# A fused attention and gated-MLP kernel: casts and copies moved to ScalarE, loads in another turn, and a first quarter of products issued one by one

## The chip, the cores and the metric

The kernel runs on one core of one Trainium2 chip. Its metric is the device time of one launch in microseconds (us), smaller is better. A core has five engines that run their own queues of instructions and wait for each other by semaphores: PE (TensorE, matrix products; PEld is its loading of weights), ACT (ScalarE), DVE (VectorE), POOL (GpSimd), and SP (SyncE), which here only issues DMAs.

## What is computed

A windowed attention with four sink keys, then an MLP with a gate, on 4 x 768 tokens of 8 heads x 64:

```
scores = q @ k.T / sqrt(64);  keep = (key < 4) or (0 <= row - key < 128)
a = softmax(where(keep, scores, -1e9));  attn = a @ v          # per batch and head
x = attn as (3072 tokens, 512)
h = x @ w_in                                                    # w_in: 512 x 2048
g = h * sigmoid(beta * h)
out = g @ w_out                                                 # w_out: 2048 x 512
```

The kernel computes in bf16 with f32 sums, and the sigmoid as a tanh: g = (tanh(beta h / 2) + 1) * h, with the half put into the last copy.

## The kernel before

**The tiling.** The tokens are cut into 8 blocks of 384 (`TT`). A *unit* n (0 to 31) is the attention of one pair of heads for one block: units 4T to 4T + 3 make the block T of x, kept turned in `xT`. A *tile* i (0 to 127) is one 128 x 384 piece of h: tile i belongs to block i // 16 and is the sum of four products (c = 0 to 3), one for each unit of its block. So "tiles 0 to 15" are block 0 and need units 0 to 3 and all of w_in; tiles 16 to 31 are block 1 and need units 4 to 7. After each tile come a tanh on ACT (`tanh`, L755) and a gate on DVE (`gate`, L769); a PSUM bank is free again when its gate is done. Tiles 4 to 15 take turns in two banks (`acc0`, `acc1`), later ones in four. The output products (`project`, L796) of block 0 begin when tile 31 has been issued, and from then on tiles and output products of neighbouring blocks are mixed.

**A unit's steps.** SP loads q, k and v (f32) into `q_stage`, `k_stage`, `v_stage`. POOL casts them to bf16 (`cast`, L490 and L493, 384 columns each). For units 0 to 11 PE turns q and k ("in", `transpose_in`, L513), and one copy of 768 columns brings them out of PSUM to `qkT` (L522). From unit 12 on a DMA does it. Then: the scores of the sink keys ("sink", L542) with an exp to `E_sink` (L545); the scores in two chunks ("a" and "b", `scores`, L569), each with an exp of 768 columns to `E` (L576) and a mask by DVE (`mask`, L587); a @ v ("av", `attend`, L685 and L696); 1/sum and its product (`normalise`, L705 and L707); and the way out to `xT` ("out", `transpose_out`: PE L724, a copy of 384 columns L728). For n below `ADDED` = 6 the mask is not multiplied by DVE but added on PE, by a product of a unit matrix with `far_a` or `far_b` ahead of the scores (L561, two products of 384 columns for a chunk).

**The weights.** w_in comes in pieces 0 to 7 of 0.5 MB (`load_w`, L473): pieces 2j and 2j + 1 hold rows c = 0, 1 and c = 2, 3 of the columns that tiles 4j to 4j + 3 of each block need. POOL casts each to bf16 (`cast_w`, L478, 1024 columns). w_out follows in eight pieces in the same buffers `wst`.

**What sets the order.** The program is recorded as nodes and a list scheduler (`Prog.order`) places them: at each step it takes, on each engine, the node that could start first by the costs given with each `op` (`busy`, `lag`), with some look ahead; ties go to the node recorded first. `P.together` makes one node of several instructions. So the order of recording, the costs and the dependencies decide every engine's queue; at run time the queues are fixed. The order of recording is a loop over slots s: slot s records tile s (0 to 31), and the steps of units whose place is s. `EARLY` gives the places of the steps of units 4 to 7 (fractions lie between tiles), `FIRST` those of units 8 on: a unit's steps are at FIRST[n] + 0, 1, 2, 3, 5, 7 (`STEPS`). SP's loads are recorded in a line: units 0 to 3, w_in pieces 0 to 3, units 4 to 7, w_in pieces 4 to 7, units 8 to 11, w_out. `at` sets the slots after which the whole loads of later units are issued. `BANK_B` and `BANK_S` say in which PSUM bank the second chunk and the sink scores of units 4 to 7 go.

A tile is recorded so:

```
def hidden(i):
    with P.together("pe"):
        for c in range(3 if i < 4 else 0, 4):
            node = hidden_matmul(i, c)
    tanh(i)
    return node
```

Tiles 0 to 3 had their products c = 0 to 2 recorded singly before, as units 0 to 2 come. Each product waits for its piece of w_in and its unit's part of xT:

```
r=[("w_in", m // 4 * 2 + c // 2), ("xT", T, c)]
```

Of the kernel before, what the change touches and what calls it, by code (L numbers as in the profile page):

```python
# [17 lines left out]
TT = 384  # L18
# [5 lines left out]
NW = 8  # L24
# [15 lines left out]
S_PIPE = 3 * NM  # L40
S_END = S_PIPE + (NT - 2) * NM

EARLY = {4: {'in': 0.2, 'sink': 3.0, 'a': 3.4, 'b': 5.0, 'av': 5.6, 'out': 8.0},
# [3 lines left out]
BANK_B = {4: 'h', 5: 's', 6: 'h', 7: 's'}  # L47
BANK_S = {4: 'h', 5: 'h', 6: 'h', 7: 'h'}

FIRST = {8: 27, 9: 33, 10: 34, 11: 38}  # L50
FIRST.update({12: 44, 13: 47, 14: 50, 15: 53, 16: 60, 17: 60})
FIRST.update({n: 68 + 8 * (n // 2 - 9) for n in range(18, NU)})
TURN = 0

XBAR, WHOLE = 12, 16

ADDED, FAR = 6, -float(1 << 20)
LATE, PAIRED = 2, 16
STEPS = {0: "in", 1: "sink", 2: "a", 3: "b", 5: "av", 7: "out"}

# [227 lines left out]
def bass_streamingllm_window__then__act_swish_beta_kernel(  # L288
# [71 lines left out]
    def pe(n):  # L360
        return {"busy": 2.5 + n / 2.4, "lag": 260.0}
# [89 lines left out]
    def load(n):  # L451
        for name in "qkv":
            if name != "v" and n < XBAR:
                load_qk(n, name)
            else:
                load_head(n, name, 0)
                load_head(n, name, 1)
# [17 lines left out]

    def cast_w(i):
        view, _, dst = w_piece(i)
        op("gp", lambda e: e.tensor_copy(dst, view), r=[("wst", i % NW)],  # L478
           w=[("w_in" if i < NW else "w_out", i % NW)], busy=985.0, lag=100.0)

    def cast(n, first=False):
        _, _, half, pb = place(n)
        z = n % NQK

        def view(name):
            return stage[name][pb][:, :, 3 * half:3 * half + 3, :].rearrange("p h c d -> p c h d")

        for x, name in enumerate("qk"):
            eng = "dve" if first and name == "k" else "gp"
            op(eng, lambda e, x=x, name=name: e.tensor_copy(qk16[z][:, x, :, :, :], view(name)),  # L490
               r=[(name + "_stage", pb, half, hh) for hh in range(2)], w=[(name + "16", z)],
               busy=451.0, lag=100.0)
        op("gp", lambda e: e.tensor_copy(v_aug[pb][:, 3 * half:3 * half + 3, :, 0:D], view("v")),  # L493
           r=[("v_stage", pb, half, hh) for hh in range(2)], w=[("v_aug", pb, half)], busy=451.0,
           lag=100.0)
        if n >= XBAR:
            op("sp", lambda e: e.dma_start_transpose(
                qkT[pb][:, half, :, :].rearrange("p w (c x) -> p (w c) x", c=3),
                qk16[z][:, :, :, :, :].rearrange("p w c h d -> p (w c h d)")),
               r=[("q16", z), ("k16", z)], w=[("qT", pb, half), ("qkT", pb, half)], dma=f"t{pb}{half}",  # L500
               **transfer(2 * TT * 256, 240, 1400.0))
# [50 lines left out]
    def scores(n, c, bank, name):  # L552
        _, _, half, pb = place(n)
        at = 0
        if n < ADDED:
            w = width(half, c)
            far, tile = (far_a, "far_a") if (half, c) == (0, 0) else (far_b, "far_b")
            first = 128 if (half, c) == (1, 0) else 0
            with P.together("pe"):
                for hh in range(2):  # L560
                    op("pe", lambda e, hh=hh, w=w: e.matmul(  # L561
                        bank[:, hh, 0:w], ident[:, :], far[:, first:first + w], start=True, stop=False,
                        skip_group_check=True), r=["ident", tile], w=[f"{name}{hh}"], **pe(w))
        with P.together("pe"):
            for kb, qb, nq in CHUNKS[half][c]:
                w = 128 * nq
                for hh in range(2):
                    rows = slice(64 * hh, 64 * hh + 64)
                    op("pe", lambda e, at=at, w=w, kb=kb, qb=qb, hh=hh, rows=rows: e.matmul(  # L569
                        bank[:, hh, at:at + w], qkT[pb][rows, kb // 3, 1, kb % 3 * 128:kb % 3 * 128 + 128],  # L570
                        qkT[pb][rows, half, 0, qb % 3 * 128:qb % 3 * 128 + w], start=n >= ADDED,
                        stop=True, skip_group_check=n < ADDED),
                       r=[("qT", pb, half), ("qkT", pb, kb // 3)], w=[f"{name}{hh}"],
                       busy=50.0 + w / 4.8, lag=260.0)
                at += w
        op("act", lambda e: e.activation(E[n % 2][:, c, :, 0:at], bank[:, 0:2, 0:at], AF.Exp,  # L576
                                         bias=0.0, scale=SCALE),
           x=[f"{name}0", f"{name}1"], w=[("E", n % 2, c)], **act(768))

    def mask(n, c):  # L580
        if n < ADDED:
            return
        half = place(n)[2]
        w = width(half, c)
        m, names = (mask_a, MASK_A) if (half, c) == (0, 0) else (mask_b, MASK_B)
        first = 128 if (half, c) == (1, 0) else 0
        op("dve", lambda e: e.tensor_tensor(  # L587
            E[n % 2][:, c, :, 0:w], E[n % 2][:, c, :, 0:w],
            m[:, first:first + w].unsqueeze(1).to_broadcast([128, 2, w]), ALU.mult),
           r=[("E", n % 2, c), *names], w=[("E", n % 2, c)], **dve(780.0))  # L590
# [153 lines left out]
    def hidden_matmul(i, c):  # L744
        T, m = i // NM, i % NM
        bank, name = hidden_bank(i)
        return op("pe", lambda e: e.matmul(  # L747
            bank, w_in16[:, c, m * 128:(m + 1) * 128], xT[:, c, T * TT:(T + 1) * TT],
            start=(c == 0), stop=(c == 3)),
           r=[("w_in", m // 4 * 2 + c // 2), ("xT", T, c)], w=[name], **pe(TT))  # L750

    def tanh(i):
        m = i % NM
# [3 lines left out]
           x=[name], r=["beta"], w=[("th", i % 3)], **act(TT + 100))  # L757

    def hidden(i):
        with P.together("pe"):  # L760
            for c in range(3 if i < 4 else 0, 4):
                node = hidden_matmul(i, c)
        tanh(i)
        return node

# [7 lines left out]
    def project_last(half, m):  # L773
        T, t = NT - 1, 2
        bank, name = (acc[0][:, 0:256], "acc0") if half == 0 else (h_ps[:, 0, 0:256], "h0")
        cols = slice(256 * half, 256 * half + 256)
        node = op("pe", lambda e: e.matmul(bank, g[T % 2][:, m, t * 128:(t + 1) * 128],
                                           w_out16[:, m, cols], start=(m == 0), stop=(m == NM - 1)),
                  r=[("g", T % 2, m), ("w_out", m // 2)], w=[name], **pe(256))
        if m == NM - 1:  # L780
            row = T * TT + t * 128
            if half == 0:
                op("act", lambda e: e.activation(out_sb[3][:, cols], bank, AF.Copy, bias=0.0,
                                                 scale=0.5), x=[name], w=[("out_sb", 3)], **act(256))
            else:
                op("dve", lambda e: e.tensor_scalar(out_sb[0][:, cols], bank, 0.5, None, ALU.mult),
                   x=[name], w=[("out_sb", 0)], **dve(330.0))
            op("sp" if half else "act", lambda e, z=3 * (1 - half): e.dma_start(
                out[row:row + 128, cols], out_sb[z][:, cols]),
               r=[("out_sb", 3 * (1 - half))], dma=f"e{half}", **transfer(128 * 256 * 4, 275))  # L790
        return node
# [3 lines left out]
    def project(T, t, m, bank, name, eng="act"):  # L795
        node = op("pe", lambda e: e.matmul(bank, g[T % 2][:, m, t * 128:(t + 1) * 128],  # L796
                                    w_out16[:, m, :], start=(m == 0), stop=(m == NM - 1)),
           r=[("g", T % 2, m), ("w_out", m // 2)], w=[name], **pe(NOUT))
        if m == NM - 1:
            z = n_out[0] % 4  # L800
            n_out[0] += 1
# [38 lines left out]
    load_w(2)  # L840
    load_w(3)
    load(4)
    load(5)
    load(6)
    load(7)
    load_w(4)
    load_w(5)
    load_w(6)
    load_w(7)
    cast(0, True)  # L850
# [57 lines left out]
        sink_keys(n, ended)  # L908


    at = {16: 38, 17: 46, 18: 52, 19: 57, 24: 69, 25: 75, 26: 81, 27: 87}
    loads = {t + 2 * x: (n, name) for n, t in at.items() for x, name in enumerate("qkv")}
    casts = {FIRST[n - 2] + (3 if n % 2 and n - 2 >= PAIRED else 1): n for n in range(10, NU)}
    casts.update({EARLY[n - 2]["sink"]: n for n in range(6, 8)})
# [1 line left out]
    for s in sorted(slots):  # L916
# [14 lines left out]
        for n, step in here:  # L931
            half = place(n)[2]
            if step == "in" and n < XBAR:
                transpose_in(n, eng="dve")
            if step == "sink" and half == 1:
                scores_sink(n, *((h_ps[:, 0, :], "h0") if BANK_S.get(n) == "h" else (s_ps[:, 0, :], "s0") if n < PAIRED
                                 else (tr_ps, "tr")))
            if step == "b" and XBAR <= n < PAIRED:
                scores_at_once(n)
# [14 lines left out]
                    later.append(lambda n=n, ended=ended: sink_keys(n, ended))  # L954
            if step == "out":
                if n < XBAR:
                    transpose_out(n, eng="act" if n < 8 else "dve")
        if s in casts:
            n = casts[s]
            cast(n)  # L960
# [100 lines left out]
```

## Time and profile before

| | us |
|---|---|
| median of 3 runs | 227.72 (225.61, 227.89, 227.72) |
| the profiled execution | 226.35 |
| its span, first to last instruction | 224.6 |
| PE busy in the span | 216.6 |
| ACT, DVE, POOL busy | 142.0, 133.3, 75.2 |
| first tanh starts (ACT) | 19.22 |
| xT of unit 7 copied, end (ACT) | 38.20 |
| first products of tiles 16 to 19 (PE) | 39.13 |
| first output product (PE) | 51.53 |

The granted clock of PE is 1.0 throughout. A product of 384 columns is shown with some 0.33 us, but four in a row start 0.162 us apart, so lengths of time are read from starts rather than from busy shares. A line of the timeline gives the start, the duration, engine, line of the code, operation, what is written and read, how many were merged (x2), and in square brackets the idle time ahead of it and what ended it.

### The profile page before, as it was taken

To read this page: it belongs to the slowest core of one execution; us is meant where nothing else is said; L and a number is where in the kernel's file an instruction comes from. 1 tells how busy PE (TensorE), PEld (TensorE's weight loads), DVE (VectorE), ACT (ScalarE), POOL (GpSimd) and SP (SyncE) were. 2 spreads that over 40 slices of the span, in tenths; PEclk is the share of its full clock that TensorE was granted. 3 is DMA by queue.
4 is the path that set the end of the run, shared out by engine and by line. 5 is a ranking of instruction groups with operands and counts; after the bars stand their busy time and mean duration, and the time that the engine had idled before them with its cause. 6 is when DMAs were issued, how large, how long until landed. Compare 5 with 4: busy or idle time off the path is not lost.

```text
span 224.6 us, 4507 instructions
## 1 busy us (share of the span) xinstructions
PE 216.6 (96%) x1732; PEld 122.5 (55%) x1753; DVE 133.3 (59%) x259; ACT 142.0 (63%) x222; POOL 75.2 (33%) x149
## 2 busy tenths in 40 slices
PE   7997999999999999999999999999999999999995
PEld 4463555655555555555465655555556565555554
DVE  5477787897766535555285566667667666254300
ACT  2674897794446666556587669566877584465410
POOL 6769569599335211444301623700000000000000
PEclk9999999999999999999999999999999999999999
DMA  6999999899999899999998999551021002111012
GB/s 186 292 330 287 270 339 288 270 392 278 142 206 221 241 229 167 277 260 190 235 238 184 227 223 182 146 136 32 32 85 64 20 9 72 50 47 47 22 74 95
DMA packets 95438, 39.80 MB, mean 177 GB/s; under 512 B 81960, under 2 KB 88376, under 8 KB 95416
## 3 DMA queue, kind: packets, MB, share of 16 engines
q1 hardware_dynamic: 93760, 38.75, 69.3%
q10 hardware_dynamic: 1656, 0.76, 1.2%
q8 instruction: 14, 0.23, 0.4%
q14 instruction: 8, 0.07, 0.1%
HBM read 27.30 MB, written 6.29 MB: 150 GB/s over the span
## 4 chain that ended last, share of the span: by engine, by line
PE 89%; DVE 4%; DMA 2%; ACT 1%; issue 1%; POOL 0%; ACTq 0%; DVEq 0%
PE acc L796 34%; PE six L747 30%; PE acc L747 6%; PE six L696 5%; PE six L642 3%; DMA v_stage<-in_v_dram 2%; PE six L569 2%; PE six L796 1%; PE six L513 1%; PE six L685 1%; PE six L542 1%; DVE g L769 1%; PE six L561 1%; DVE v_sink L891 1%; DVE qkT L522 1%
## 5 line engine op out<-in xcount | busy, mean ns | idle before, releaser
L796 PE MATMUL acc<-w_out,g 128*128 128x512 bf16 x332 | 84.4, 379 | 0.9
L755 ACT ACTIVATE th<-six,beta_half 128x384 f32<-128x384 f32 x106 | 61.1, 582 | 30.5 <-PE six L747 25.2
L747 PE MATMUL six<-xT,w_in 128*128 128x384 bf16 x424 | 78.1, 326 | 0.1
L769 DVE SCALAR_TENSOR_TENSOR g<-th,six 128x384 bf16<-128x384 f32 x106 | 57.2, 551 | 28.9 <-ACT th L755 25.9
L747 PEld LDWEIGHTS six<-xT,w_in 128*128 128x128 bf16 x424 | 40.4, 98 | 29.1 <-ACT E L613 0.7
L796 PEld LDWEIGHTS acc<-w_out,g 128*128 128x128 bf16 x352 | 32.9, 98 | 33.9 <-issue 1.8
L662 DVE TENSOR_TENSOR E<-E,mask_all 128x1536 bf16<-128x1536 bf16 x20 | 19.4, 972 | 30.1 <-ACT E L654 24.8
L654 ACT ACTIVATE E<-six 128x1536 bf16<-128x1536 f32 x16 | 22.3, 1448 | 10.6 <-PE six L642 10.6
L490 POOL CAST qk<-q_stage 128x384 bf16<-128x384 f32 x32 | 17.7, 554 | 29.8 <-DMA q_stage<-in_q_dram 17.0
L576 ACT ACTIVATE E<-six 128x768 bf16<-128x768 f32 x24 | 18.8, 810 | 9.3 <-PE six L569 9.3
L493 POOL CAST v_aug<-v_stage 128x384 bf16<-128x384 f32 x32 | 16.7, 532 | 16.2 <-DMA v_stage<-in_v_dram 9.6
L490 POOL CAST qk<-k_stage 128x384 bf16<-128x384 f32 x31 | 16.5, 532 | 16.3 <-DMA k_stage<-in_k_dram 16.2
L804 ACT ACTIVATE out_sb<-acc 128x512 f32<-128x512 f32 x22 | 12.9, 598 | 12.4 <-PE acc L796 12.2
L696 PEld LDWEIGHTS six<-v_aug,E 128*128 128x128 bf16 x384 | 17.0, 97 | 4.3 <-POOL v_aug L493 0.7
L696 PE MATMUL six<-v_aug,E 128*128 128x65 bf16 x384 | 18.9, 193 | 0.5 <-POOL v_aug L493 0.3
L707 DVE TENSOR_TENSOR o_norm<-six,rden 128x384 bf16<-128x384 f32 x32 | 17.8, 557 | 1.4
L747 PE MATMUL acc<-xT,w_in 128*128 128x384 bf16 x88 | 16.8, 327 | 1.2 <-DVE g L769 1.2
L755 ACT ACTIVATE th<-acc,beta_half 128x384 f32<-128x384 f32 x22 | 12.7, 583 | 5.6 <-PE acc L747 4.9
L769 DVE SCALAR_TENSOR_TENSOR g<-th,acc 128x384 bf16<-128x384 f32 x22 | 11.7, 551 | 3.7 <-ACT th L755 3.3
L747 PEld LDWEIGHTS acc<-xT,w_in 128*128 128x128 bf16 x88 | 7.9, 98 | 7.0 <-DVE g L769 2.1
L478 POOL CAST w_in<-wst 128x1024 bf16<-128x1024 f32 x8 | 9.0, 1129 | 6.1 <-DMA wst<-in_moe_w_in_dram 5.8
L522 DVE COPY qkT<-six 128x768 bf16<-128x768 bf16 (+1 forms) x10 | 9.1, 913 | 2.4 <-PE six L513 2.4
(72 smaller groups left out, 156.7 us busy)
## 6 DMA issues: line engine op xcount, KB each, us to landing
out_dram<-out_sb SPq DMA_DIRECT2D x23, 256.0 KB, 2.6
wst<-in_moe_w_in_dram SPq DMA_DIRECT2D x8, 512.0 KB, 6.4
wst<-in_moe_w_out_dram SPq DMA_DIRECT2D x8, 512.0 KB, 7.7
q_stage<-in_q_dram SPq DMA_DIRECT2D x8, 384.0 KB, 4.2
k_stage<-in_k_dram SPq DMA_DIRECT2D x8, 384.0 KB, 3.9
v_stage<-in_v_dram SPq DMA_DIRECT2D x8, 384.0 KB, 4.0
v_stage<-in_v_dram SPq DMA_DIRECT2D x30, 96.0 KB, 3.9
q_stage<-in_q_dram SPq DMA_DIRECT2D x12, 192.0 KB, 5.0
```

The source lines that it names most:

```text
L490: op(eng, lambda e, x=x, name=name: e.tensor_copy(qk16[z][:, x, :, :, :], view(name)), r=[(name + "_stage", pb, half, hh) for hh in range( ...
L493: op("gp", lambda e: e.tensor_copy(v_aug[pb][:, 3 * half:3 * half + 3, :, 0:D], view("v")), r=[("v_stage", pb, half, hh) for hh in range(2 ...
L576: op("act", lambda e: e.activation(E[n % 2][:, c, :, 0:at], bank[:, 0:2, 0:at], AF.Exp, bias=0.0, scale=SCALE), x=[f"{name}0", f"{name}1"] ...
L654: op("act", lambda e, u=u, first=first: e.activation(E[u % 2][:, :, :, :].rearrange("p c h x -> p (c h x)"), six[:, first:first + 3, :].re ...
L662: op("dve", lambda e: e.tensor_tensor(both, both, mask_all[:, half, :].unsqueeze(1).to_broadcast([128, 2, 768]), ALU.mult), r=[("E", z, 0) ...
L696: last=(x == len(kbs) - 1): e.matmul(av_ps[:, at + hh * D1:at + hh * D1 + D1], E[z][:, c, h2, col:col + 128], v_aug[pb][:, kb, hh, :], sta ...
L707: op("dve", lambda e: e.tensor_tensor(o_norm[o][:, :, :, :].rearrange("p m h d -> p (m h) d"), src[:, :, 0:D], rden[z][:, :].unsqueeze(2). ...
L747: return op("pe", lambda e: e.matmul(bank, w_in16[:, c, m * 128:(m + 1) * 128], xT[:, c, T * TT:(T + 1) * TT], start=(c == 0), stop=(c == 3)),
L755: op("act", lambda e: e.activation(th[i % 3][:, :], bank, AF.Tanh, bias=0.0, scale=beta_half[:, m:m + 1]), x=[name], r=["beta"], w=[("th", ...
L769: op("dve", lambda e: e.scalar_tensor_tensor(g[T % 2][:, m, :], th[i % 3][:, :], 1.0, bank, ALU.add, ALU.mult), r=[("th", i % 3)], x=[name ...
L796: node = op("pe", lambda e: e.matmul(bank, g[T % 2][:, m, t * 128:(t + 1) * 128], w_out16[:, m, :], start=(m == 0), stop=(m == NM - 1)), r ...
L804: op("act", lambda e: e.activation(out_sb[z][:, :], bank, AF.Copy, bias=0.0, scale=0.5), x=[name], w=[("out_sb", z)], **act(NOUT))
```

## The change

- **Casts.** Of w_in pieces 0, 2, 3, 5 and 7, ACT now casts one half (512 columns, the odd c) and POOL the other. Products wait for their own half.
- **Copies.** The turned q and k of units 4, 5, 7, 8, 9, 10 and 11 are copied out of PSUM by ACT (768 columns each), of unit 6 by DVE; before, DVE copied all. On the way out, ACT copies units 5, 7, 8 and 11, DVE units 4, 6, 9 and 10; before, ACT copied units 4 to 7 and DVE 8 to 11.
- **Loads.** SP's line is now unit 4, piece 4, unit 5, piece 5, units 6 and 7, pieces 6 and 7.
- **Tiles 4 to 19** are recorded product by product, so that the scheduler may put other work between a tile's products and start those whose unit is there.
- **Places.** Units 4 to 7 get new places and banks; units 8 to 11 start 8 to 9 slots earlier, units 12 to 15 2 to 7 slots earlier, later ones shift by at most one; some whole loads shift by up to 3 slots.
- **Masks.** Added on PE for units 0 to 3 and three chunks more (11 chunks; before, units 0 to 5, 12 chunks).
- **Planner costs** of POOL's casts are raised (985 to 1080, 451 to 530).

Cut to its core:

```
-EARLY = {4: {'in': 0.2, 'sink': 3.0, 'a': 3.4, 'b': 5.0, 'av': 5.6, 'out': 8.0},
-         5: {'in': 2.4, 'sink': 3.8, 'a': 3.8, 'b': 6.6, 'av': 6.8, 'out': 9.6},
-         6: {'in': 3.9, 'sink': 6.9, 'a': 7.0, 'b': 8.0, 'av': 14.7, 'out': 15.0},
-         7: {'in': 6.9, 'sink': 13.2, 'a': 13.2, 'b': 14.0, 'av': 14.8, 'out': 15.7}}
-BANK_B = {4: 'h', 5: 's', 6: 'h', 7: 's'}
-BANK_S = {4: 'h', 5: 'h', 6: 'h', 7: 'h'}
-FIRST = {8: 27, 9: 33, 10: 34, 11: 38}
-FIRST.update({12: 44, 13: 47, 14: 50, 15: 53, 16: 60, 17: 60})
-FIRST.update({n: 68 + 8 * (n // 2 - 9) for n in range(18, NU)})
+EARLY = {4: {'in': -3.0, 'sink': -0.9, 'a': -2.8, 'b': 3.7, 'av': 6.8, 'out': 11.6},
+         5: {'in': 0.1, 'sink': 4.0, 'a': 4.0, 'b': 5.3, 'av': 8.3, 'out': 14.7},
+         6: {'in': 4.0, 'sink': 8.9, 'a': 9.2, 'b': 10.1, 'av': 13.3, 'out': 13.6},
+         7: {'in': 5.0, 'sink': 10.0, 'a': 13.2, 'b': 13.8, 'av': 15.4, 'out': 15.9}}
+BANK_B = {4: 'h', 5: 'h', 6: 'h', 7: 'h'}
+BANK_S = {4: 's', 5: 't', 6: 'h', 7: 's'}
+TURN_IN = {4: 'act', 5: 'act', 6: 'dve', 7: 'act', 8: 'act', 9: 'act', 10: 'act', 11: 'act'}
+TURN_OUT = {4: 'dve', 5: 'act', 6: 'dve', 7: 'act', 8: 'act', 9: 'dve', 10: 'dve', 11: 'act'}
+APART = 20
+HALVED = (0, 2, 3, 5, 7)
+FIRST = {8: 19, 9: 24, 10: 26, 11: 29}
+FIRST.update({12: 37, 13: 44, 14: 48, 15: 51, 16: 60, 17: 60})
+FIRST.update({n: (69, 76, 83, 92, 99, 108, 115)[n // 2 - 9] for n in range(18, NU)})
-ADDED, FAR = 6, -float(1 << 20)
+ADDED = {*((n, c) for n in range(4) for c in range(2)), (4, 1), (5, 0), (7, 1)}
...
     def cast_w(i):
+        if i in HALVED:
+            n = 1
+            op("act", lambda e: e.copy(dst[:, n:], view[:, n:]), r=[("wst", i % NW)], w=[(name, i % NW, 1)],
+               **act(512))
+            op("gp", lambda e: e.tensor_copy(dst[:, 0:n], view[:, 0:n]), r=[("wst", i % NW)],
+               w=[(name, i % NW, 0)], busy=600.0, lag=100.0)
+            return
...
-           r=[("w_in", m // 4 * 2 + c // 2), ("xT", T, c)], w=[name], **pe(TT))
+           r=[("w_in", m // 4 * 2 + c // 2, c % 2), ("xT", T, c)], w=[name], **pe(TT))
...
     def hidden(i):
-        with P.together("pe"):
-            for c in range(3 if i < 4 else 0, 4):
-                node = hidden_matmul(i, c)
+        for cs in ((3,),) if i < 4 else ((0,), (1,), (2,), (3,)) if i < APART else (range(4),):
+            with P.together("pe"):
+                for c in cs:
+                    node = hidden_matmul(i, c)
...
     load(4)
+    load_w(4)
     load(5)
+    load_w(5)
     load(6)
     load(7)
-    load_w(4)
-    load_w(5)
     load_w(6)
     load_w(7)
...
-    at = {16: 38, 17: 46, 18: 52, 19: 57, 24: 69, 25: 75, 26: 81, 27: 87}
+    at = {16: 38, 17: 43, 18: 49, 19: 56, 24: 70, 25: 76, 26: 83, 27: 88}
...
-                transpose_in(n, eng="dve")
+                transpose_in(n, eng=TURN_IN.get(n, "dve"))
...
-                    transpose_out(n, eng="act" if n < 8 else "dve")
+                    transpose_out(n, eng=TURN_OUT.get(n, "dve"))
```

More of the change, by code (lines that the diff above doesn't have):

```diff
@@ L41 @@
 S_END = S_PIPE + (NT - 2) * NM
-EARLY = {4: {'in': 0.2, 'sink': 3.0, 'a': 3.4, 'b': 5.0, 'av': 5.6, 'out': 8.0},
[3 rows of a table removed]
-BANK_B = {4: 'h', 5: 's', 6: 'h', 7: 's'}
-BANK_S = {4: 'h', 5: 'h', 6: 'h', 7: 'h'}
-FIRST = {8: 27, 9: 33, 10: 34, 11: 38}
-FIRST.update({12: 44, 13: 47, 14: 50, 15: 53, 16: 60, 17: 60})
-FIRST.update({n: 68 + 8 * (n // 2 - 9) for n in range(18, NU)})
+EARLY = {4: {'in': -3.0, 'sink': -0.9, 'a': -2.8, 'b': 3.7, 'av': 6.8, 'out': 11.6},
[3 rows of a table added]
+BANK_B = {4: 'h', 5: 'h', 6: 'h', 7: 'h'}
[7 more added lines that the diff above has]
+FIRST.update({n: (69, 76, 83, 92, 99, 108, 115)[n // 2 - 9] for n in range(18, NU)})
 TURN = 0
 XBAR, WHOLE = 12, 16
-ADDED, FAR = 6, -float(1 << 20)
+ADDED = {*((n, c) for n in range(4) for c in range(2)), (4, 1), (5, 0), (7, 1)}
+FAR = -float(1 << 20)
 LATE, PAIRED = 2, 16
@@ L477, in cast_w @@
         view, _, dst = w_piece(i)
+        name = "w_in" if i < NW else "w_out"
+        if i in HALVED:
[5 more added lines that the diff above has]
+            return
         op("gp", lambda e: e.tensor_copy(dst, view), r=[("wst", i % NW)],
-           w=[("w_in" if i < NW else "w_out", i % NW)], busy=985.0, lag=100.0)
+           w=[(name, i % NW, 0), (name, i % NW, 1)], busy=1080.0, lag=100.0)
     def cast(n, first=False):
@@ L491, in cast @@
                r=[(name + "_stage", pb, half, hh) for hh in range(2)], w=[(name + "16", z)],
-               busy=451.0, lag=100.0)
+               busy=530.0, lag=100.0)
         op("gp", lambda e: e.tensor_copy(v_aug[pb][:, 3 * half:3 * half + 3, :, 0:D], view("v")),
-           r=[("v_stage", pb, half, hh) for hh in range(2)], w=[("v_aug", pb, half)], busy=451.0,
+           r=[("v_stage", pb, half, hh) for hh in range(2)], w=[("v_aug", pb, half)], busy=530.0,
            lag=100.0)
@@ L554, in scores @@
         at = 0
-        if n < ADDED:
+        if (n, c) in ADDED:
             w = width(half, c)
@@ L570, in scores @@
                         bank[:, hh, at:at + w], qkT[pb][rows, kb // 3, 1, kb % 3 * 128:kb % 3 * 128 + 128],
-                        qkT[pb][rows, half, 0, qb % 3 * 128:qb % 3 * 128 + w], start=n >= ADDED,
-                        stop=True, skip_group_check=n < ADDED),
+                        qkT[pb][rows, half, 0, qb % 3 * 128:qb % 3 * 128 + w], start=(n, c) not in ADDED,
+                        stop=True, skip_group_check=(n, c) in ADDED),
                        r=[("qT", pb, half), ("qkT", pb, kb // 3)], w=[f"{name}{hh}"],
@@ L580, in mask @@
     def mask(n, c):
-        if n < ADDED:
+        if (n, c) in ADDED:
             return
@@ L778, in project_last @@
                                            w_out16[:, m, cols], start=(m == 0), stop=(m == NM - 1)),
-                  r=[("g", T % 2, m), ("w_out", m // 2)], w=[name], **pe(256))
+                  r=[("g", T % 2, m), ("w_out", m // 2, m % 2)], w=[name], **pe(256))
         if m == NM - 1:
@@ L797, in project @@
                                     w_out16[:, m, :], start=(m == 0), stop=(m == NM - 1)),
-           r=[("g", T % 2, m), ("w_out", m // 2)], w=[name], **pe(NOUT))
+           r=[("g", T % 2, m), ("w_out", m // 2, m % 2)], w=[name], **pe(NOUT))
         if m == NM - 1:
@@ L933, in bass_streamingllm_window__then__act_swish_beta_kernel @@
             if step == "in" and n < XBAR:
-                transpose_in(n, eng="dve")
+                transpose_in(n, eng=TURN_IN.get(n, "dve"))
             if step == "sink" and half == 1:
-                scores_sink(n, *((h_ps[:, 0, :], "h0") if BANK_S.get(n) == "h" else (s_ps[:, 0, :], "s0") if n < PAIRED
+                scores_sink(n, *((h_ps[:, 0, :], "h0") if BANK_S.get(n) == "h" else (tr_ps, "tr") if BANK_S.get(n) == "t" else (s_ps[:, 0, :], "s0") if n < PAIRED
                                  else (tr_ps, "tr")))
```

## The prediction

> **What bounds the kernel now.** I read the page first (busy time, slices), then the sums by stage, then the timeline from 13 to 52 us, engine by engine. Starts and durations are in us, idle time ahead of an instruction in square brackets.
>
> ```profile
> PE 216.6 (96%) x1732; PEld 122.5 (55%) x1753; DVE 133.3 (59%) x259; ACT 142.0 (63%) x222; POOL 75.2 (33%) x149
> ```
>
> PE looks full, but a product's end is modelled, so I went by starts: four 384-column products in a row take 0.65, or 0.162 each, and what lies beyond that between two starts is lost. By this count every loss of more than 0.15 after 52 us is the pause of 0.2 to 0.3 around scores, a missing record, or a few such; PE is the bound there. Ahead of 52 us the losses sum to some 7.3: 2.7 before 17 us, 4.6 after. What a change of the start can win lies in these 4.6, of which about 1.2 is the pause around scores.
>
> ```profile
> 0.00:20.00 20.00, 17.62 (x163) 10.15 (x163) 11.40 (x30) 10.28 (x17) 14.23 (x36) 1.00 0.93 275
> 20.00:40.00 20.00, 18.24 (x192) 10.77 (x193) 16.34 (x32) 17.12 (x31) 14.53 (x25) 1.00 0.99 292
> 40.00:52.00 12.00, 11.95 (x93) 7.13 (x93) 10.91 (x21) 10.16 (x18) 9.88 (x15) 1.00 0.98 345
> 52.00:67.00 15.00, 14.80 (x131) 7.49 (x131) 10.30 (x22) 6.06 (x9) 8.10 (x16) 1.00 0.98 192
> ```
>
> The columns are the stage, its length, then PE, PEld, DVE, ACT, POOL busy (instructions), clock, DMA share, GB/s. From 20 to 52 us ACT is at 85%, DVE at 85%, and the DMA engines are full: the loads land as fast as they can. From 52 to 67 ACT has 9 us free.
>
> ```profile
> 16.05 0.47 ACT L728 COPY xT<-acc 128x384 bf16<-128x384 bf16 x1
> 19.22 1.05 ACT L755 ACTIVATE th<-acc,beta_half 128x384 f32<-128x384 f32 x2 [2.70 <-PE acc L747]
> ...
> 37.73 0.47 ACT L728 COPY xT<-six 128x384 bf16<-128x384 bf16 x1
> ```
>
> ACT idles 2.70 ahead of the first tanh; the last of the four copies that make xT of units 4 to 7 ends at 38.20, and only then can the second quarter of tiles (16 on) be finished.
>
> ```profile
> 28.96 1.04 POOL L478 CAST w_in<-wst 128x1024 bf16<-128x1024 f32 x1 [2.61 <-DMA wst<-in_moe_w_in_dram]
> 30.31 1.16 POOL L478 CAST w_in<-wst 128x1024 bf16<-128x1024 f32 x1 [0.31 <-DMA wst<-in_moe_w_in_dram]
> 32.21 1.17 POOL L478 CAST w_in<-wst 128x1024 bf16<-128x1024 f32 x1 [0.75 <-DMA wst<-in_moe_w_in_dram]
> 33.77 1.04 POOL L478 CAST w_in<-wst 128x1024 bf16<-128x1024 f32 x1 [0.38 <-PE six L696]
> ```
>
> Pieces 4 to 7 of w_in are cast as they land, so tiles 8 and 9 wait until 30.9.
>
> ```profile
> 37.83 1.47 PE L747 MATMUL acc<-xT,w_in 128*128 128x384 bf16 x8 [0.40 <-DVE g L769]
> 39.13 1.14 PE L747 MATMUL six<-xT,w_in 128*128 128x384 bf16 x6
> ```
>
> At 39.13 the tiles of the second quarter start. The first output product is at 51.53; the rest, 173.1 to the end of the 224.6 span, is PE's. So the question is when PE reaches that product, and with how much done. The profiled execution took 226.35 (span plus 1.75); the median of the three is 227.72, 0.6% above, their spread 1.0%. My sum is against 226.35.
>
> **The change, part by part.** Prices are steps from one start to the next in a row of like instructions: tanh 0.475 (two in 1.05, one 0.58), exp of 768 0.70 (two in 1.51, one 0.81), E_sink 0.375, xT copy 0.37, gate 0.47.
>
> *Up to 20.4 us: three half casts on ACT.* Half a piece on ACT (512 columns) is not in the trace; the nearest row, an output copy of 512, is 0.60 (0.49 a step). Bounds 0.4 and 1.0. Pieces 2 and 3 fall into the idle 2.70, piece 0 into the 0.77 idle ahead of unit 3's exps; nothing is queued that they delay unless piece 3 lands after 18.6 (POOL began it at 18.66 without waiting). POOL saves 5 x 0.43 = 2.1 in all (384 columns take 0.51, 1024 1.04, so half takes 0.62). Cost 0, bounds -0.3 and +0.5.
>
> *Loads.* SP issues w_in piece 4 ahead of units 5 to 7 (12 DMAs go behind it) and piece 5 ahead of units 6 and 7 (8 DMAs). A piece is 0.524 MB, at 292 GB/s 1.8. Unit 7's v was cast at 25.84 as it landed: now 25.8 + 3.6 = 29.4, unit 6's 24.0 + 3.6, unit 5's 22.3 + 1.8. Piece 4 comes at about 22.4 instead of 28.9, piece 5 at 26.4 instead of 30.3. The bytes up to piece 7 are the same. POOL's queue has the half of piece 5 ahead of unit 6's casts, which land after it anyway.
>
> *ACT from the first tanh to xT of unit 7.* Before: 16 tanh, 8 exps, 4 E_sink, 4 xT copies = 7.6 + 5.6 + 1.5 + 1.5 = 16.2, spread over 20.7. After: two xT copies move to DVE (-0.7), three turned q and k of 768 come (its 384 form takes ACT 0.48; by the exps' step 0.70 each, bounds 0.70 and 0.96, twice the 384 form: +2.1) and two half casts (+1.0): 18.5, so not before 37.7. DVE loses those copies (0.95 each) and is not the limit. In this queue the half of piece 5 waits for its landing at 26.4, where ACT arrives at about 25.7; behind it stand tanh 7, E_sink and two exps of unit 5, and PE waits for bank acc1 behind that tanh. I walked the rest by these prices: unit 7 turned at 30.7, its exps at 35.3 to 36.8, its av behind tiles 13 and 14, its xT at 40.3, 2.1 later than now.
>
> *Product by product.* Tiles 16 to 19 now issue 12 of their 16 products before that xT: 12 x 0.162 = 1.95. No instruction is added. So tile 19 ends where it did (41.7): +0.15, bounds -3.4 (the waits gone) and +2.5.
>
> *Added masks.* 11 chunks instead of 12 get the mask on PE: -2 x 0.163 = -0.3; DVE gets one mask more (0.56 to 0.8), hidden by its idle time.
>
> *Units 8 to 11 earlier.* Unit 9's scores, unit 8's way out and unit 10's turning move ahead of the first output product: 0.84 of PE and 0.5 of pauses, taken back later. ACT between tile 16's tanh and tile 31's gets 16 tanh, 4 exps, 3 turned copies, an xT copy = 12.9, where before it had 9.0 (16 tanh, 2 exps). PE needs 11.0 for the same stretch, but ends it two tiles and several ACT instructions ahead of tile 31's tanh: 41.0 + 8.7 to tanh 27, 1.2 for it and its gate, 0.7 for tile 31, is 51.6, against PE's own 41.7 + 11.0 = 52.7. Both near full, I add 0.45 for mixed waits, bounds 0 and 1.5.
>
> *The rest.* FIRST of units 12 to 35 and the whole loads move by up to 7 places; PE stays full there with scores in other gaps. 0, bounds -0.3 and +0.5.
>
> Sum: 226.35 + 0 + 0.15 - 0.3 + 0.45 + 0 = 226.65. No change.
>
> A rule against it: in the Trainium skill, "ScalarE: Activation LUTs", *Rules for kernel authors*, gives simple elementwise arithmetic to VectorE rather than ScalarE, as up to about three times as fast in bf16, and a copy is work of that kind. The trace's turned copies of 384 say otherwise: ACT 0.48, DVE 0.56, both from PSUM. The row decides; the rule stands behind the last rival. The second: "SBUF — State Buffer", *Reading the diagram*, says only VectorE and GpSimd lock each other out and ScalarE waits for nobody. The trace agrees in part (piece 1's cast took 1.52 instead of 1.04 beside VectorE's v_sink copies); piece 1 stays whole, so the sum is the same.
>
> **Rivals.**
> *Faster: the waits go.* If piece 5 lands by 25.7 and unit 7's chain is not behind ACT's queue, xT stands by 38.2 and PE has 12 products in hand: 4.6 less 1.2 of pauses, 3.4 won: 226.35 - 3.4 + 0.2 = 223.1. For it: POOL's waits of 2.61 and 0.75, tiles 8 and 9 idle until 30.9. Against: ACT's 18.5 in 18.5.
> *Slower: ACT becomes the bound.* The copy of piece 5's half is at the head of ACT's queue when it is not there. Each us after 26.4 goes through to unit 7's xT and to tile 31. It decides from 2.3 late on; were the piece as late as piece 4 is now (28.9), 2.5: 226.65 + 2.5 = 229.1. For it: all DMA engines full. Against: 6.7 MB are in by about 24.4 at the slices' rates, and pieces of w_in were cast some 2.0 after their bytes were in.
> *Slower: ACT copies at a third of DVE's speed.* Were a turned copy of 768 to take 2.85 (three times DVE's 0.95) instead of 0.80, three of them in a full queue: 226.65 + 3 x 2.05 = 232.8. For it: no copy of 768 on ACT is in the trace. Against: the 0.48 of its 384 form.
>
> **How the numbers follow.** Forecast 0.52, its own range 224.7 to 228.3 (its smaller bounds); waits gone 0.27 (222.8 to 224.4); ACT bound 0.19; slow copies 0.02. Leaving out the last and the far ends, 223.2 to 229.4 holds eight in ten. One per cent, 2.3 us, is about what a measurement of this kernel can tell from no change: below 224.1 lies most of the second case and none of the first, 0.25; above 228.6 most of the third and the last, 0.19; between, 0.56. I predict 226.6.
>
> **What would show it.** Right: ACT over 90% busy from 20 to 52 us; POOL's cast of piece 4 near 22.4 and ACT's half of piece 5 near 26.4; xT of unit 7 copied at about 40, with products of tiles 16 to 19 ahead of it; the first output product at 52.0 to 53.5. Wrong, faster: xT of unit 7 by 38.5 and the first output product before 50.5 with the same work done. Wrong, slower: ACT waits of over 1 us for w_in's DMA, or a turned copy of over 1 us, and PE's starts apart by the same.

## The result, and the profile after

The changed kernel takes 225.46 us (median of 19 runs, 224.88 to 226.53) against 226.73 for the kernel before (median of 19 runs, the three above among them): a ratio of 0.9951, 95% interval 0.9934 to 0.9968 (the plain quotient of the medians is 0.9944). Measured once more in the last group of experiments, as `again`, it stood at 0.9982 (0.9967 to 0.9997). So the change wins 0.4 to 1.1 us by the two ratios, and 0.1 to 1.5 by the ends of their intervals: the forecast, 226.6 and no change within 1%, holds, and the sign was not seen. Its profiled span is 223.1 us, 1.5 below the one before.

The page's first part and the sums by stage, of the changed kernel (columns as before: length, PE, PEld, DVE, ACT, POOL, clock, DMA share, GB/s):

```profile
PE 215.2 (96%) x1730; PEld 122.2 (55%) x1751; DVE 128.2 (57%) x253; ACT 147.3 (66%) x234; POOL 73.9 (33%) x149
```

```profile
20.00:40.00 20.00, 19.21 (x199) 11.56 (x198) 15.24 (x32) 18.45 (x35) 12.58 (x23) 1.00 1.01 295
40.00:52.00 12.00, 11.83 (x99) 6.63 (x98) 10.98 (x21) 11.94 (x23) 10.79 (x16) 1.00 1.02 348
52.00:67.00 15.00, 14.69 (x136) 7.80 (x137) 7.96 (x17) 8.29 (x12) 9.33 (x17) 1.00 0.73 162
```

ACT went from 17.12 to 18.45 of 20 us and from 10.16 to 11.94 of 12 (18.91 and 11.48 in the second profile, whose start is later). The DMA engines, full from 52 to 67 us before, have room there. The reason is open: it is not the loads of units 8 to 11, which had been issued by 38.5 us in both kernels.

ACT's timeline ahead of the first tanh, around the copy of piece 5's half, and of the last xT copies:

```profile
17.61 0.62 ACT L489 CAST w_in<-wst 128x512 bf16<-128x512 f32 x1 [0.81 <-DMA wst<-in_moe_w_in_dram]
18.55 1.05 ACT L771 ACTIVATE th<-acc,beta_half 128x384 f32<-128x384 f32 x2 [0.32 <-PE acc L763]
...
24.26 0.88 ACT L538 COPY qkT<-six 128x768 bf16<-128x768 bf16 x1
24.93 0.72 ACT L489 CAST w_in<-wst 128x512 bf16<-128x512 f32 x1
25.45 0.69 ACT L771 ACTIVATE th<-acc,beta_half 128x384 f32<-128x384 f32 x1
...
36.84 0.48 ACT L744 COPY xT<-six 128x384 bf16<-128x384 bf16 x1 [0.45 <-PE six L740]
...
38.31 0.48 ACT L744 COPY xT<-six 128x384 bf16<-128x384 bf16 x1 [0.24 <-PE six L740]
```

Of the idle 2.70 ahead of the first tanh, 0.81 ahead of piece 3's half and 0.32 ahead of the tanh are left. The half of piece 5 starts without a wait in brackets. From the first tanh to 35.58, for 17.0 us, no line of ACT has a wait in brackets, and in the second profile of the same kernel it is the same 17.0 us (19.80 to 36.82). Then come waits of 0.17 to 0.47, all ended by PE, among them those ahead of the last two xT copies.

POOL's casts of pieces 4, 5, 6 and 7, and of unit 7's v between them (all fell on a landing):

```profile
20.85 1.04 POOL L494 CAST w_in<-wst 128x1024 bf16<-128x1024 f32 x1 [0.75 <-DMA wst<-in_moe_w_in_dram]
...
24.06 0.62 POOL L491 CAST w_in<-wst 128x512 bf16<-128x512 f32 x1 [0.80 <-DMA wst<-in_moe_w_in_dram]
...
27.75 0.51 POOL L509 CAST v_aug<-v_stage 128x384 bf16<-128x384 f32 x1 [0.39 <-DMA v_stage<-in_v_dram]
29.90 1.04 POOL L494 CAST w_in<-wst 128x1024 bf16<-128x1024 f32 x1 [1.63 <-DMA wst<-in_moe_w_in_dram]
31.25 0.61 POOL L491 CAST w_in<-wst 128x512 bf16<-128x512 f32 x1 [0.31 <-DMA wst<-in_moe_w_in_dram]
```

PE where the last xT is awaited:

```profile
36.64 1.30 PE L763 MATMUL acc<-xT,w_in 128*128 128x384 bf16 x7
37.78 0.33 PE L763 MATMUL six<-xT,w_in 128*128 128x384 bf16 x1
37.94 0.33 PE L740 MATMUL six<-ident,o_norm 128*128 128x128 bf16 x3
38.11 0.65 PE L763 MATMUL six<-xT,w_in 128*128 128x384 bf16 x3
38.72 0.99 PE L763 MATMUL acc<-xT,w_in 128*128 128x384 bf16 x5
```

Unit 7 is turned for the way out at 37.94, its xT is there at 38.79, and PE has products of tiles 16 to 19 to issue on both sides of that.

**Where the time came from.** The absolute start is partly chance. The first tanh comes at 19.22 in the profile of before, and at 18.55 in the changed kernel's, but at 18.78 to 19.80 in the eleven other profiles of kernels made from it, whose loads up to piece 3 are issued in the same order, and at 18.34 in o_loads_apart, made from the kernel before. So I count from the first tanh. The columns are its own time, then the time from it to the last product of the first 80 (tiles 0 to 19), from there to the first output product, from there to the end of the span, and the sum of the three; "ratio" is the timed one against before.

| kernel | first tanh | to tile 19 | to first output product | to the end | sum | ratio (95% interval) |
|---|---|---|---|---|---|---|
| before | 19.22 | 22.35 | 9.96 | 173.09 | 205.40 | 1 |
| changed | 18.55 | 21.15 | 11.60 | 171.84 | 204.60 | 0.9951 (0.9934, 0.9968) |
| changed, again | 19.80 | 21.14 | 11.39 | 172.32 | 204.85 | 0.9982 (0.9967, 0.9997) |
| u_halves | 19.58 | 22.24 | 11.55 | 172.14 | 205.93 | 1.0032 (1.0013, 1.0050) |
| u_apart | 18.98 | 23.00 | 11.00 | 172.15 | 206.15 | 1.0046 (1.0028, 1.0063) |
| u_turns | 19.05 | 23.48 | 12.93 | 170.98 | 207.40 | 1.0052 (1.0032, 1.0073) |
| u_masks | 19.30 | 22.62 | 11.61 | 172.41 | 206.63 | 1.0048 (1.0024, 1.0072) |
| u_places | 19.62 | 21.13 | 9.70 | 174.61 | 205.44 | 0.9990 (0.9976, 1.0004) |
| k_loads | 19.22 | 29.73 | 11.39 | 172.32 | 213.43 | 1.0334 (1.0307, 1.0362) |
| x_act_20 | 19.19 | 22.69 | 11.39 | 172.32 | 206.39 | 1.0028 (1.0007, 1.0049) |
| x_act_40 | 19.14 | 21.13 | 13.25 | 172.05 | 206.43 | 1.0044 (1.0026, 1.0063) |
| x_dve_20 | 18.78 | 22.12 | 11.39 | 172.31 | 205.81 | 1.0034 (1.0016, 1.0052) |
| c_out | 18.99 | 21.13 | 11.55 | 172.14 | 204.82 | 0.9980 (0.9959, 1.0002) |
| o_loads_apart | 18.34 | 23.54 | 10.96 | 172.51 | 207.01 | 1.0068 (1.0048, 1.0087) |

Of the 1.47 us between the two spans, 0.67 is the earlier first tanh, and the second profile, with the tanh at 19.80 and a span of 224.6, shows that it does not belong to the change. (Ahead of that run I had expected a ratio of 0.993 to 0.998, a first tanh at about 19.2 and 204.6 from it to the end; it gave 0.9982, 19.80 and 204.85.) The other 0.80 (0.55 in the second profile) is: 1.2 won up to tile 19, 1.4 to 1.6 lost up to the first output product, and 0.8 to 1.25 got back after it, because units 8 to 10 are further on by then. The kernel before has one profile only, so these differences rest on one reading of it. The way to tile 19 repeats to 0.02 us in the five profiles in which those queues were not touched or hardly (21.13 to 21.15), whatever the start, as ACT's 17.0 us without a wait do, so a difference of 0.2 there can be read.

### The profile page after: what moved, and what is told of

It is laid out like the page before. It is cut to its first block, busy times and chain, and to the rows that moved or that the text cites. A ratio compares the mean times of both kernels' runs of the same rounds, so it can differ in the third digit from the quotient of the medians.

```text
span 223.1 us, 4496 instructions
## 1 busy us (share of the span) xinstructions
PE 215.2 (96%) x1730; PEld 122.2 (55%) x1751; DVE 128.2 (57%) x253; ACT 147.3 (66%) x234; POOL 73.9 (33%) x149
## 4 chain that ended last, share of the span: by engine, by line
PE 83%; SPq 10%; DMA 2%; issue 2%; POOL 1%; DVE 0%; ACT 0%; DVEq 0%; POOLq 0%
PE acc L813 33%; PE six L763 30%; PE six L712 4%; SPq L447 4%; SPq L455 4%; PE acc L763 3%; PE six L658 3%; DMA wst<-in_moe_w_in_dram 2%; SPq L481 2%; PE six L813 2%; PE six L585 1%; PE six L701 1%; PE six L558 1%; PE six L622 1%; PE six L794 1%
## 5 line engine op out<-in xcount | busy, mean ns | idle before, releaser
L763 PE MATMUL six<-xT,w_in 128*128 128x384 bf16 x424 | 80.7, 326 | 0.2
L509 POOL CAST v_aug<-v_stage 128x384 bf16<-128x384 f32 x32 | 17.6, 565 | 20.8 <-DMA v_stage<-in_v_dram 11.7
L592 ACT ACTIVATE E<-six 128x768 bf16<-128x768 f32 x24 | 19.4, 838 | 4.1 <-PE six L585 4.0
L763 PE MATMUL acc<-xT,w_in 128*128 128x384 bf16 x88 | 18.0, 327 | 0.6 <-DVE g L786 0.5
L561 ACT ACTIVATE E_sink<-six 128x384 bf16<-128x384 f32 x16 | 8.2, 513 | 5.4 <-PE six L558 4.6
L721 DVE RECIPROCAL rden<-six 128x6 f32<-128x6 f32 x32 | 6.1, 191 | 5.5 <-PE six L712 5.5
```

Source lines behind the costliest of these rows:

```text
L763: return op("pe", lambda e: e.matmul(bank, w_in16[:, c, m * 128:(m + 1) * 128], xT[:, c, T * TT:(T + 1) * TT], start=(c == 0), stop=(c == 3)),
```

## The experiments

Two theories. Mine: PE's lag ahead of the first output product sets the end, ScalarE is the tightest engine there, and the loads and the products in hand cover what ScalarE makes late. The rivals: the half casts or the VectorE copies by themselves are the gain, or any delay on the chain of engines goes through, whichever engine it is on. In the u_ runs, o_loads_apart and, in a few places, c_out the planner sorts the queues anew, so an undone part comes with other queues; k_loads and the x_ runs keep every other queue as it was.

**u_halves**

```
-HALVED = (0, 2, 3, 5, 7)
+HALVED = ()
```

> The changed kernel with no piece of w_in halved (POOL casts all eight whole; the planner orders the rest anew). Theory, ScalarE nearly full from 20 to 52 us so that the half casts buy nothing there: 0.993 to 0.997 of before, as the changed kernel has (0.995). Rival, the gain comes from w_in being ready sooner through two engines: 0.998 to 1.003, with POOL's casts later by 0.4 us a piece and tiles waiting for them.

Measured 1.0032, and 1.1 us more up to tile 19. The theory's numbers fail, and the rival's upper end is just passed: the half casts are worth keeping in this plan. The rival's reason is not borne out, though. Piece 4 is cast whole in both kernels. Piece 5, cast whole by POOL from 24.40 to 25.44, is ready 5.9 us after the first tanh; in the changed kernel POOL's half is ready after 6.1 and ACT's after 7.1. What comes later without halves is xT of unit 7, 21.5 us after the first tanh against 20.2. Why the new order does that is open.

**k_loads**: SP's turn undone, all other queues kept.

```
-unit 4, piece 4, unit 5, piece 5, unit 6, unit 7, piece 6, piece 7
+unit 4, unit 5, unit 6, unit 7, piece 4, piece 5, piece 6, piece 7
```

> The changed kernel with SP's loads in the old turn (units 5 to 7 ahead of pieces 4 and 5), every other queue exactly as in the changed kernel. Theory, the turn of the loads has to go with the other queues: POOL and ScalarE now wait for pieces 4 and 5, some 5 and 4 us later than in the changed kernel, less what the queues have in hand: slower than before, 1.00 to 1.02. Rival, the loads are hidden either way: 0.993 to 0.998.

Measured 1.0334, well over the range. POOL's queue, and PE's, show why:

```profile
28.39 1.04 POOL L499 CAST w_in<-wst 128x1024 bf16<-128x1024 f32 x1 [7.48 <-DMA wst<-in_moe_w_in_dram]
29.37 0.51 POOL L511 CAST qk<-q_stage 128x384 bf16<-128x384 f32 x1
```

```profile
23.68 0.33 PE L563 MATMUL six<-qkT,k_sink 128*128 128x384 bf16 x1
29.94 0.50 PE L534 MATMUL six<-ident,qk 128*128 128x128 bf16 x3 [5.93 <-POOL qk L511]
```

```profile
24.00:28.00 4.00, 0.01 (x1) 0.00 (x0) 0.70 (x2) 1.11 (x3) 0.00 (x0) 0.70 0.94 253
28.00:32.00 4.00, 2.06 (x11) 1.37 (x12) 0.00 (x0) 0.89 (x2) 3.61 (x7) 0.50 1.02 355
32.00:36.00 4.00, 4.00 (x33) 2.20 (x31) 1.21 (x3) 2.58 (x5) 4.00 (x9) 0.52 1.05 296
```

POOL stands 7.48 us at the head of its queue for piece 4, with unit 5's casts behind it, so PE waits 5.93, and PE's granted clock stands at 0.50 and 0.52 from 28 to 36 us. The loads are not hidden: their turn and the queues' order have to go together. It is POOL's queue, not ScalarE's as in my slower rival, that blocks first.

**u_apart**

```
-APART = 20
+APART = 4
```

> The changed kernel with tiles 4 to 19 again in one piece each (the planner orders the rest anew). Theory, the products of tiles 16 to 19 issued ahead of the last xT are 1.95 us of PE work that covers the wait for it: 0.997 to 1.004. Rival, they cover nothing: 0.993 to 0.997.

Measured 1.0046, just over the theory's upper end, which its interval holds. PE at the same place:

```profile
37.90 0.33 PE L740 MATMUL six<-ident,o_norm 128*128 128x128 bf16 x3
39.11 0.34 PE L740 MATMUL six<-ident,o_norm 128*128 128x128 bf16 x3 [0.88 <-ACT xT L744]
39.29 1.72 PE L763 MATMUL acc<-xT,w_in 128*128 128x384 bf16 x8
```

Where the changed kernel issues products, PE now idles 0.88, and all 16 products of tiles 16 to 19 come after it. Up to tile 19 it takes 1.85 longer. Not all of that is the missing cover: in this order unit 7's xT itself comes 0.74 later after the first tanh (21.0 against 20.2), which leaves 1.1.

**x_act_20, x_act_40, x_dve_20**: four additional instructions of 512 columns, all other queues kept. In short:

```
     op("act", tanh of tile i)
+    if i in (4, 7, 10, 13):          # x_act_40: (16, 20, 24, 28)
+        op("act", lambda e: e.copy(out_sb[3][:, :], far_b[:, :]), after=the tanh, busy=0.0, lag=0.0)
+        # x_dve_20: op("dve", ... e.tensor_tensor(out_sb[3], far_b, far_b, ALU.mult))
```

> The changed kernel with four more ScalarE copies of 512 columns (some 0.5 us each, 2.0 in all; into a buffer that is not used yet) behind the tanh of tiles 4, 7, 10 and 13, no other queue changed. Theory, ScalarE is the tightest engine from 20 to 40 us (18.45 of 20 busy): 1 to 2 us longer than the changed kernel, 0.999 to 1.004 of before. Rival, PE or the loads set the time there: under 0.5 us longer, 0.994 to 0.997.

> The changed kernel with four more ScalarE copies of 512 columns behind the tanh of tiles 16, 20, 24 and 28 (2.0 us in all), no other queue changed. ScalarE is busy 11.94 of 12 us from 40 to 52 there, with overlaps. Theory, it is the tightest engine there too: 1 to 2 us longer than the changed kernel, 0.999 to 1.004 of before. Rival, PE is: under 0.5 us longer, 0.994 to 0.997.

> The changed kernel with four more VectorE products of 512 columns behind the gates near tiles 4, 7, 10 and 13, no other queue changed. Theory, VectorE has room from 20 to 40 us (15.2 of 20 busy) where ScalarE has none: under 0.8 us longer than the changed kernel, where the same count on ScalarE cost 1.8. Rival, every wait on this chain of engines goes through, whichever engine it is on: 1.3 to 2.0 longer.

One such copy in x_act_20 and the sums by stage of x_act_40 and x_dve_20:

```profile
22.21 0.65 ACT L776 CAST out_sb<-far_b 128x512 f32<-128x512 bf16 x1
22.71 0.62 ACT L772 ACTIVATE th<-acc,beta_half 128x384 f32<-128x384 f32 x1
```

```profile
40.00:52.00 12.00, 10.94 (x87) 5.75 (x85) 9.44 (x18) 12.00 (x24) 11.10 (x17) 1.00 1.02 352
```

```profile
20.00:40.00 20.00, 18.66 (x190) 10.83 (x190) 17.61 (x35) 18.14 (x33) 14.11 (x23) 1.00 1.03 303
```

A copy takes 0.51 from its start to the next, four are 2.0 us of ScalarE. In the traces 1.54 of them go through up to tile 19 (76%), and 1.86 of the later four up to the first output product (over the second profile's 11.39: 92%, with ACT at 12.00 of 12). VectorE's four took 1.07, 0.60, 1.05 and 0.60 from start to start, 3.3 in all, longer than I had meant; 0.98 of them went through (30%). So the traces agree that ScalarE is the tightest engine, more so from 40 to 52 us. VectorE's room is smaller than I had said: 0.98 is over the 0.8 of x_dve_20's theory and under the 1.3 of its rival, and the last section shows that its four products held up POOL as well. The timed ratios do not separate the two engines: against the second measurement of the changed kernel x_act_20 is 1.0 us longer, x_dve_20 1.2, each by 0.5 to 0.6 either way. x_act_40, 1.4 longer, is just over its range.

**u_turns, u_masks, u_places, o_loads_apart**

```
u_turns:   -TURN_IN = {4: 'act', ...}     +TURN_IN = {}; TURN_OUT = {4 to 7: 'act'}
u_masks:   -ADDED = {units 0 to 3, (4, 1), (5, 0), (7, 1)}   +ADDED = {units 0 to 5}
u_places:  FIRST and at as before
o_loads_apart: the kernel before, with only the new turn of the loads and tiles 4 to 19 product by product
```

> The changed kernel with all turned q and k copied by VectorE and the way out as before (the planner orders the rest anew). Theory, these copies only move between two engines that are both near full: 0.993 to 0.999. Rival, VectorE at 0.95 us a copy was what the first 52 us hung on: 1.000 to 1.006. Second rival, ScalarE is the bound and is relieved by 4.2 us: 0.988 to 0.992.

> The changed kernel with the mask added on PE for both chunks of units 0 to 5 (12 chunks) as before. Theory: 0.3 us more on PE and one mask less on VectorE: 0.995 to 0.998. Rival, the masks' waits matter more than the products: 0.990 to 0.994, or over 0.998.

> The changed kernel with units 8 on in their old places (and the whole loads after their old slots); units 4 to 7 as changed. Theory, from tile 20 on PE is full and it does not matter where the units stand: 0.993 to 0.997, as the changed kernel. Rival, bringing units 8 to 11 forward keeps PE full where it waited: 0.998 to 1.003. Second rival, it overloads ScalarE from 40 to 52 us: 0.989 to 0.992.

> The kernel before with two parts of the change alone: the new turn of the loads, and tiles 4 to 19 product by product (the planner orders the rest anew, with the old places of units 4 to 7). Theory, these two carry the gain only with places that fit: 0.996 to 1.006. Rival, they are the gain: 0.993 to 0.997.

u_turns measured 1.0052, as its first rival said; o_loads_apart 1.0068, just above the theory's range; u_masks 1.0048, over its theory's 0.998, where its rival has no upper end. None of these losses can be given to the part alone. The chunk put back on PE is 0.33 us of products, yet tile 19 comes 1.5 later; the planner had sorted the queues anew. The five undone parts other than the loads cost about 1.1, 1.4, 1.6, 1.5 and 0.2 us against the second measurement, 5.8 in all, of a gain of 0.4 to 1.1: they do not add up, and the places fit this set of parts only. What u_halves, u_apart, u_turns and u_masks share is a later xT of unit 7, 21.0 to 22.2 us after the first tanh against 20.2, and more idle time of ScalarE on the way to tile 19: 2.4 to 4.2 us in all, where both profiles of the changed kernel have 1.55. So in these traces it is the order of the queues that costs, and not ScalarE's amount of work. u_places (0.9990) lies in its rival's range and overlaps the changed kernel's second measurement: by stage it ends the stretch to the first output product 1.7 to 1.9 sooner and gives 2.3 to 2.8 back, so bringing units 8 on forward is worth 0.6 to 0.8 in the trace and nothing that the timing tells.

**c_out**: the way out of units 5 and 7 on VectorE.

```
-TURN_OUT = {4: 'dve', 5: 'act', 6: 'dve', 7: 'act', 8: 'act', 9: 'dve', 10: 'dve', 11: 'act'}
+TURN_OUT = {4: 'dve', 5: 'dve', 6: 'dve', 7: 'dve', 8: 'act', 9: 'dve', 10: 'dve', 11: 'act'}
```

> The changed kernel with the way out of units 5 and 7 copied by VectorE instead of ScalarE (0.74 us less on ScalarE from 20 to 40 us, the output products' banks in slightly other turn). Theory, ScalarE is the tightest engine there: 0.3 to 0.7 us shorter than the changed kernel, 0.990 to 0.995 of before. Rival, the last xT is on a chain of single latencies and VectorE's gates delay it: 0.995 to 1.000.

Measured 0.9980, like the changed kernel beside it (0.9982), and 21.13 to tile 19 as there: the theory's 0.3 to 0.7 did not come, and the ratio lies in the rival's range. Those two copies stand where ScalarE waits for PE anyway (0.45 and 0.24 idle), so a tight engine was relieved at the one place where it had time. No version here beats the changed kernel by more than the measurement tells.

## Why the prediction was right, point by point

**No change, by a sum of small terms: right,** and one term of it mis-sized. Counted from the first tanh, 205.4 became 204.6 and 204.85, so -0.8 and -0.55; the sum had +0.3. The signs of being right were given in absolute times, and with these the start, which is chance, decides: the second profile meets them (piece 4 cast at 22.30, ACT's half of piece 5 at 26.18, xT of unit 7 at 40.03, the first output product at 52.33), the first misses them by 1.2 to 1.6, and by 0.7 at the output product (20.85, 24.93, 38.79, 51.31). So I go by distances from the first tanh.

**Up to 20.4 us, 0: right.** The halves took 0.61 to 0.64 on POOL and ACT at the start (0.62 and 0.60 expected), but for POOL's half of piece 2, which took 1.15 beside VectorE's v_sink copies (14.52 to 16.00; 0.62 in the second profile); ACT's lie in its idle time; what moved was the landing of the first loads, issued in the same order in both kernels and 0.6 either way between executions. Piece 3 was cast by ACT at 17.61 or 19.27 in two profiles of the same kernel, and the first tanh followed 0.94 and 0.53 later.

**The loads' landings: the step that failed, by its size.** I had piece 4 at 3.2 us after the first tanh, piece 5 at 7.2, unit 7's v at 10.2. Measured: 2.3 and 2.5; 5.5 and 5.5; 9.2 and 9.5 (two profiles). Two things were off. I took 1.8 us a piece from the mean rate of 292 GB/s over 20 to 40 us; from the landing of unit 4's v to that of piece 4 it was 1.26 and 1.25, and the slices from 11 to 22 us of the changed kernel run at 374 and 333. And the 22.4 is 1.8 after unit 4's v in the kernel before, whose cast stood in POOL's queue and did not wait for a landing (no bracket):

```profile
20.57 0.51 POOL L493 CAST v_aug<-v_stage 128x384 bf16<-128x384 f32 x1
```

How much of the error each of the two made was not separated. So ScalarE did not wait for piece 5 (it came to it at 24.93, with POOL on the same piece since 24.06), unit 7's exps began at 33.54, 15.0 after the first tanh instead of 16.1, and its xT was there 20.2 after it instead of 21.1.

**"So tile 19 ends where it did: +0.15": -1.2,** inside its bounds. xT of unit 7 is later than before (20.2 after the first tanh against 19.0), as forecast, and the products in hand cover more than that: by 38.79, when it was copied, PE had issued 74 of the first 80 products, so at least ten of the sixteen of tiles 16 to 19 where I had twelve, and it did not wait for the copy. Without the cover u_apart takes 1.85 longer, where I had 1.95; but 0.74 of it is the later xT there, so the near agreement is partly luck.

**Units 8 to 11 earlier: right in size against the kernel before.** 11.45 forecast from tile 19 to the first output product, 11.60 and 11.39 measured; 1.3 forecast to come back, 1.25 and 0.77 measured. "Both near full" is borne out by ACT's 11.94 of 12 (11.48 in the second profile) and by x_act_40. That the earlier places cost 0.45 in the end is not: with the old places u_places needs 0.6 to 0.8 more in the trace, all of it behind tile 19.

**Masks, -0.3: not tested cleanly,** since the queues moved with it. **The rest:** the units end at 31, not at 35; nothing hangs on it.

**The rivals.** *Waits go*: a third of its gain came (1.2 of 3.4), but not by its path, as xT of unit 7 stood later after the first tanh and not earlier. *ACT becomes the bound*: its condition, a late piece 5, did not occur; k_loads shows that a piece standing ahead of its landing at the head of a queue passes on, at a price over the 2.5 that I gave it. *Copies at a third of VectorE's speed*: no. A turned copy of 768 took ScalarE 0.79 to 0.88, VectorE's took 0.95. The Trainium skill ("ScalarE: Activation LUTs", *Rules for kernel authors*) gives its factor of up to about three for `relu`, `max`, `min`, `add` and `mul` with one source in bf16; to carry it over to these copies out of PSUM was my step, and the trace does not bear it out.

## What to carry to other kernels

When PE, ScalarE and VectorE are all above 80% busy in a start-up stage, as here from 20 to 52 us, moving work between them may change little. Here it helped to let PE issue the products that were ready ahead of the last input, and what that covers can be counted beforehand. The turn of the loads and the order of the queues that consume them are one decision: a queue whose head waits for a late load stops all that stands behind it. Where the start depends on landings, compare profiles from a point after them, and run the same kernel twice before a difference of half a per cent is explained.

## What was not expected of the hardware

- The first loads can land 1.65 us apart between executions with the same queue: POOL's first cast of w_in starts at 12.34 and 13.99 in the two profiles of the changed kernel. The first tanh moved with it, by 1.25.
- In k_loads PE's granted clock fell from 1.00 to 0.50 between 25 and 26 us, in the middle of PE's wait of 5.93 us (24.01 to 29.94), and came back only between 35 and 36 us, some 6 us after PE had work again. The way to tile 19 was 8.6 longer in all.
- A VectorE product of two bf16 inputs of 512 columns took 0.60 or 1.05 to 1.07 us from start to start. The trace of x_dve_20 tells why:

```profile
20.84 1.04 POOL L495 CAST w_in<-wst 128x1024 bf16<-128x1024 f32 x1 [0.74 <-DMA wst<-in_moe_w_in_dram]
21.27 1.15 DVE L776 TENSOR_TENSOR out_sb<-far_b 128x512 f32<-128x512 bf16 x1
21.82 0.96 POOL L507 CAST qk<-q_stage 128x384 bf16<-128x384 f32 x1
...
26.14 0.51 POOL L507 CAST qk<-q_stage 128x384 bf16<-128x384 f32 x1
26.51 0.68 DVE L776 TENSOR_TENSOR out_sb<-far_b 128x512 f32<-128x512 bf16 x1
26.65 0.91 POOL L507 CAST qk<-k_stage 128x384 bf16<-128x384 f32 x1
```

Each of the four began while a POOL cast was running and ended 0.54 to 0.60 after that cast's end (21.88 and 22.42, 26.65 and 27.19): it was slow when the cast had long to go. The POOL cast behind each took 0.91 to 0.96 instead of 0.51. So the two engines held each other up in these places.
